# Three quarters of one weight block loaded as 20 rows by a transfer of its own

## The chip, the cores and the metric

The kernel runs on one core of a Trainium2 chip. The metric is device time in microseconds (us) of one launch. Arrays are laid out on the host beforehand; that layout is not part of the time. Everything is float32.

## What is computed

One decoding step for 8 sequences with a model width of 512. A layer norm of `x` feeds two branches: attention of 32 query heads over a cache with 8 key and value heads of 4096 positions, and a small gated MLP whose output, through a silu, multiplies the attention's output. The change touches the last product of the MLP, `z1 * g` (8 x 896) times `w_out` (896 x 512).

```python
def _B_ref(x, w_in, w_sp, b_sp, w_out):
    z = _gelu(jnp.einsum("bsd,df->bsf", x, w_in))
    z1 = z[..., :Fh]
    z2 = _layernorm(z[..., Fh:], axis=-1)
    g = jnp.einsum("ts,bsf->btf", w_sp, z2) + b_sp[None, :, None]
    return jnp.einsum("bsf,fd->bsd", z1 * g, w_out)

x = A_x
xn = _layernorm(x, axis=-1)
s = _A_ref(xn, A_k_cache, A_v_cache, A_wq, A_wo)
g = _silu(_B_ref(xn, B_w_in, B_w_sp, B_b_sp, B_w_out))
return x + s * g
```

`_A_ref` is softmax attention: queries `xn @ wq`, keys and values from the caches, then the product with `wo`. The caches are 8 x 8 x 4096 x 128 each, 134 MB each, and are read once.

## The kernel before

**Data in.** Three buffers of 128 partitions x 64 KB, `slot_A`, `slot_B` and `slot_C`, take everything large. All large loads are issued by SyncE (SP) in the order of the program: `wq` into B (8 MB, L338), `w_mlp` into C (L341), then for each of the eight key/value heads the two halves of the keys into A and B (L547, 8 MB each) and the two halves of the values into C and B (L553). In the last head the first half of the values goes into A, C takes `wo` (L558) in seven pieces that get smaller, and the second half of the values comes in two parts. `x` comes in two pieces on ScalarE's queue (L335): each is 8 rows of 1152 bytes. SP issues a load once the engines that read the old contents of its buffer are done; SP keeps its order, so a load behind a waiting one waits too.

**`w_mlp`.** 128 rows of 10752 numbers: first `w_in` (L342), then the seven blocks of `w_out` side by side (L343), each 128 rows x 512 columns.

**Order of the work.** A small recorder writes down every operation, finds which must wait for which, and emits each engine's program: heads 0 to 6 as a loop on TensorE (PE), the other engines unrolled. Before the heads stand `project_q` twice (L415 to L423, queries from `wq`) and `mlp` (from L431). In `mlp`, PE multiplies by `w_in` (L437); VectorE (DVE), ScalarE and GpSimd make the gelu, the layer norm and the gate (L441 to L467); two transposes (L470) and a copy (L471) bring the hidden vector into `hT`; seven matrix products with the blocks of `w_out` (L474) accumulate in the four row groups of the bank `sc`; DVE copies the result (L476) and the rest makes `gate`. Block j is added in row group j mod 4, so the last block, j = 6, goes to group 2.

**After `mlp`.** Each head computes scores from the keys in A and then in B (L506), softmax (L510 to L529), and the products with the values (L538, with L540, L541 and L544 behind each sequence). The load of the first values into C (L553) may be issued once the last product with `w_out` is done, since they take that buffer's place.

**The end.** The last head folds in the product with `wo` (L566, L574); the last of the seven pieces is awaited by the last 16 matrix products of L574, after which two DVE operations (L630, L631) and the store of the result (L632) remain.

Of the kernel before, what the change touches and what calls it, by code (L numbers as in the profile page):

```python
# [15 lines left out]
P = 128  # L16
B, D = 8, 512
HKV, REP, S, DH = 8, 4, 4096, 128
NK = D // P
G = 4  # L20
J = S // (G * P)
R = 32
FH = 896
FQ = 256
NB = FH // P
# [13 lines left out]
E = 2  # L39
W = P // E  # L40
BANK = 512


class Region:


    def __init__(self, ap):
# [10 lines left out]
        if str(ap.space) == "PSUM" or "PSUM" in str(ap.space):  # L58
            self.p0, self.p1 = 0, P
            banks = np.unique(at // BANK)  # L60
            at = (banks[:, None] * BANK + np.arange(BANK)[None, :]).reshape(-1)
        at = np.unique(at)
# [254 lines left out]
        return self.rec.add(self.eng, "tensor_tensor", (out, a, b), {"op": ALU.subtract})  # L317


def gqa_gmlp_decode(real, x, kT, v, wq, wo, w_mlp, out):  # L320
    nc = Recorder(real)

    def sb(name, shape, **kw):
        return real.alloc_sbuf_tensor(name, shape, F32, **kw).ap()

    def psum(name, shape):
        return real.alloc_psum_tensor(name, shape, F32).ap()

    slots = {n: sb(f"slot_{n}", [P, SLOT], align_bytes=ALIGN) for n in "ABC"}
    pbuf = sb("pbuf", [P, J * P])  # L330
    tbuf = sb("tbuf", [P, B * J * G * REP])
# [5 lines left out]

    nc.sync.dma_start(slots["B"], wq, key="B")  # L338
    wq_sb = slots["B"].rearrange("p (k n) -> p k n", k=NK)
    n_in, n_mlp = NK * 2 * FH, NK * 2 * FH + NB * D  # L340
    nc.sync.dma_start(slots["C"][:, :n_mlp], w_mlp, key="C")  # L341
    w_in_sb = slots["C"][:, :n_in].rearrange("p (k n) -> p k n", k=NK)  # L342
    w_out_sb = slots["C"][:, n_in:n_mlp].rearrange("p (j d) -> p j d", d=D)  # L343

    ident = sb("ident", [P, P])
    make_identity(nc, ident)
# [27 lines left out]
    def shift(t, i):  # L374
        lo = (E - 1 - i) * B
        return t[:, lo:lo + R]

    sc = psum("sc", [P, 2, 512])
    o_ps = [psum(f"o_ps{i}", [P, G, DH]) for i in range(2)]
    po = psum("po", [P, 512])[:, :B * REP]  # L380
    scr = [psum(f"scr{i}", [P, 512]) for i in range(3)]
# [17 lines left out]
    for i in range(E):  # L399
        for g in range(G):  # L400
            lo = g * P + i * W
            nc.tensor.matmul(px[R * g:R * (g + 1), :W], shift(same8, i)[:B], x_sb[:, lo:lo + W],
                             start=(i == 0), stop=(i == E - 1))
# [21 lines left out]
    def mlp():  # L425
        zu = pbuf.rearrange("p (a f) -> p a f", f=FQ)
        z, u = zu[:, :2], zu[:, 2:]
        hT = tbuf[:, :2 * P].rearrange("p (a s) -> p a s", a=2)
        y_sb, e = tbuf[:, 2 * P:2 * P + D], zu[:, 2, :W]
        pz = scr[1]  # L430
        nc.vector.memset(pz, 0.0)  # L431
        for part in range(2):
            for k in range(NK):
                for g in range(G):
                    lo = g * FQ
                    n = min(FQ, FH - lo)
                    nc.tensor.matmul(pz[R * g:R * (g + 1), part * FQ:part * FQ + n], xnT[:, k, :],  # L437
                                     w_in_sb[:, k, part * FH + lo:part * FH + lo + n],
                                     start=(k == 0), stop=(k == NK - 1))
        zf, uf = z.rearrange("p a f -> p (a f)"), u.rearrange("p a f -> p (a f)")  # L440
        nc.vector.tensor_copy(zf, pz)  # L441
        nc.vector.tensor_mul(uf, zf, zf)
        nc.vector.tensor_scalar(uf, uf, 0.044715, 1.0, op0=ALU.mult, op1=ALU.add)
        nc.vector.tensor_mul(uf, uf, zf)
        nc.scalar.activation(uf, uf, AF.Tanh, scale=GELU_C)
        nc.vector.tensor_scalar(uf, uf, 1.0, 0.5, op0=ALU.add, op1=ALU.mult)
        nc.vector.tensor_mul(zf, uf, zf)

        def mean(src, pm, name):
            part_sum, t = sb(f"{name}_sum", [P, 1]), sb(name, [P, 1])  # L450
            nc.vector.tensor_reduce(part_sum, src, op=ALU.add, axis=AX.X)
            nc.tensor.matmul(pm, same_all, part_sum, start=True, stop=True)
            nc.vector.tensor_scalar(t, pm, 1.0 / FH, None, op0=ALU.mult)
            return t

        z1, z2 = z[:, 0, :], z[:, 1, :]
        mu = mean(z2, scr[0][:, :1], "mu")
        nc.vector.tensor_scalar(z2, z2, mu, None, op0=ALU.subtract)
        nc.vector.tensor_mul(u[:, 0, :], z2, z2)
        nc.vector.memset(u[(G - 1) * R:, 0, FH - (G - 1) * FQ:], 0.0)  # L460
        var = mean(u[:, 0, :], scr[2][:, :1], "var")
        nc.vector.tensor_scalar(var, var, EPS, None, op0=ALU.add)
        rs = sb("rs", [P, 1])
        nc.gpsimd.tensor_tensor(rs, var, neg_half, op=ALU.pow)
        nc.vector.tensor_scalar(z2, z2, rs, None, op0=ALU.mult)
        nc.vector.tensor_scalar(z2, z2, wb[:, 0:1], wb[:, 1:2], op0=ALU.mult, op1=ALU.add)
        nc.vector.tensor_mul(u[:, 1, :], z2, z1)  # L467
        th = scr[0][:, :2 * P]
        for a in range(2):
            nc.tensor.transpose(th[:, a * P:(a + 1) * P], u[:, 1, a * P:(a + 1) * P], ident)  # L470
        nc.vector.tensor_copy(hT.rearrange("p a s -> p (a s)"), th)  # L471
        for j in range(NB):
            g = j % G
            nc.tensor.matmul(sc[R * g:R * (g + 1), 0, :], hT[:, j % 2, R * (j // 2):R * (j // 2 + 1)],  # L474
                             w_out_sb[:, j, :], start=(j < G), stop=(j + G >= NB))
        nc.vector.tensor_copy(y_sb, sc[:, 0, :])  # L476
        py = scr[2][:, :W]
        for i in range(E):
            for g in range(G):
                lo = g * P + i * W  # L480
                nc.tensor.matmul(py[R * g:R * (g + 1), :], shift(same8, i), y_sb[:, lo:lo + W],
                                 start=(i == 0), stop=(i == E - 1))
        nc.vector.tensor_scalar(e, py, -1.0, 87.0, op0=ALU.mult, op1=ALU.min)
        nc.scalar.activation(e, e, AF.Exp)
        nc.vector.tensor_scalar(e, e, 1.0, None, op0=ALU.add)
        nc.vector.reciprocal(e, e)
        nc.vector.tensor_mul(gate, py, e)
# [7 lines left out]
    p = pbuf.rearrange("p (j s) -> p j s", j=J)  # L495
# [112 lines left out]
    project_q(0)  # L608
    project_q(1)
    mlp()  # L610
    nc.meet("tensor")
    for h in range(LOOPED):
# [9 lines left out]
    for i in range(E):  # L622
        for g in range(G):
            lo = g * P + i * W
            nc.tensor.matmul(acc[R * g:R * (g + 1), :], shift(same8, i), part_sb[:, lo:lo + W],
                             start=False, stop=False)
# [38 lines left out]
```

## Time and profile before

| what | value |
|---|---|
| time, median of 3 runs | 678.63 us (678.46 to 678.76) |
| the profiled execution, first to last instruction | 677.3 us |
| read from HBM | 290.74 MB |
| PE busy, DVE busy | 375.2 us (55%), 167.5 us (25%) |
| last load: issue to landing | 628.26 us to 674.72 us |

The span is that of one profiled execution; the median of the runs, with what lies around the span, is 1.3 us longer, and differences are carried from the one to the other. A row "DMA" gives the mean busy share of the core's 16 DMA engines, the units that move the bytes. Queues are named q1, q8 and so on: q1 are the loads from SP, q10 those from ScalarE, and the two of the kind "instruction" bring the engines' own programs. Such a row has packets, megabytes and the share of 16 engines' time. In a row "DMA packets ... under 512 B n" for a stretch of time without stores, the packets under 512 bytes are the 4-byte ones by which each DMA engine reports that its share of a transfer is done: their number is the number of engines that came to an end in that stretch.

### The profile page before, as it was taken

The page shows a single profiled execution, that of the slowest core. Times are in us where ns is not written, and L with a number is a line of the kernel's source. Part 1 is how long each engine was busy: PE and PEld are TensorE (multiplying, and loading weights), DVE is VectorE, ACT ScalarE, POOL GpSimd, SP SyncE. Part 2 cuts the span into 40 slices and gives each one's busy share as a digit, 9 for nine tenths or more (in the row PEclk, how much of TensorE's full clock was granted, in tenths as well). Part 3 has the DMA queues.
Part 4 walks back from the last instruction along what each step waited for, and adds up shares of the span by engine and source line. Part 5 has one row for each costly group of instructions (what it writes and reads, how often), then busy time and mean ns, then how long its engine had stood idle before and what let it go on. Part 6 is the DMA issues. An engine that isn't in the chain of part 4 may idle for free. (4 is left out here: it accounts for less than half of the span.)

```text
span 677.3 us, 5857 instructions
## 1 busy us (share of the span) xinstructions
PE 375.2 (55%) x2658; PEld 119.5 (18%) x2658; DVE 167.5 (25%) x277; ACT 13.4 (2%) x27; POOL 2.8 (0%) x14
## 2 busy tenths in 40 slices
PE   0547554546665455456755454655654465655657
PEld 0122121112111111111211121211211121111212
DVE  2141042302430033401521024401432024400342
ACT  0000000000000000000000000000000000000000
POOL 1000000000000000000000000000000000000000
PEclk9967666878767678877766678887676678766697
DMA  8999999999999999999999999999999999999997
GB/s 373 449 434 434 433 434 433 434 433 433 433 433 433 433 433 433 434 433 433 433 433 433 433 434 433 433 433 437 437 437 437 433 437 445 433 437 434 404 423 318
DMA packets 6233, 290.90 MB, mean 429 GB/s; under 512 B 832, under 2 KB 848, under 8 KB 1360
## 3 DMA queue, kind: packets, MB, share of 16 engines
q1 hardware_dynamic: 6192, 290.75, 99.3%
q8 instruction: 7, 0.11, 0.1%
q10 hardware_dynamic: 32, 0.02, 0.0%
q14 instruction: 2, 0.02, 0.0%
HBM read 290.74 MB, written 0.03 MB: 429 GB/s over the span
## 5 line engine op out<-in xcount | busy, mean ns | idle before, releaser
L506 PE MATMUL sc<-slot_B,qz 128*32 128x512 f32 x512 | 74.4, 746 | 76.6 <-PEq L506 76.6
L538 PE MATMUL o_ps<-slot_B,tbuf 128*16 128x512 f32 x512 | 77.5, 732 | 70.5 <-PEq L538 61.6
L506 PE MATMUL sc<-slot_A,qz 128*32 128x512 f32 x512 | 74.4, 746 | 47.6 <-PEq L506 47.6
L540 DVE TENSOR_TENSOR o_all<-o_ps,diag 128x512 f32<-128x512 f32 x64 | 44.3, 691 | 161.0 <-PE o_ps L538 161.0
L538 PE MATMUL o_ps<-slot_C,tbuf 128*16 128x512 f32 x448 | 67.0, 739 | 20.5 <-PEq L538 20.5
L510 DVE TENSOR_REDUCE nm<-sc 128x1 f32<-128x1024 f32 x8 | 9.8, 1224 | 269.5 <-PE sc L506 269.5
L541 DVE TENSOR_REDUCE o_sb<-o_all 128x128 f32<-128x512 f32 x64 | 67.8, 1060 | 2.2
L506 PEld LDWEIGHTS sc<-slot_B,qz 128*32 128x32 f32 x512 | 20.4, 134 | 130.5 <-issue 130.5
L506 PEld LDWEIGHTS sc<-slot_A,qz 128*32 128x32 f32 x512 | 20.7, 133 | 94.8 <-issue 94.8
L544 PE MATMUL po<-fold,o_sb 128*128 128x4 f32 x128 | 25.6, 270 | 12.3 <-PEq L544 12.3
L544 PEld LDWEIGHTS po<-fold,o_sb 128*128 128x128 f32 x128 | 20.3, 199 | 68.5 <-issue 64.2
L538 PEld LDWEIGHTS o_ps<-slot_B,tbuf 128*16 128x16 f32 x512 | 13.4, 106 | 100.5 <-issue 90.2
L538 PEld LDWEIGHTS o_ps<-slot_C,tbuf 128*16 128x16 f32 x448 | 13.7, 112 | 57.0 <-issue 56.8
L528 PE MATMUL scr<-ident,pbuf 128*128 128x128 f32 x64 | 14.8, 409 | 10.6 <-PEq L528 9.3
L511 ACT ACTIVATE pbuf<-sc,nm 128x1024 f32<-128x1024 f32 x8 | 8.9, 1114 | 556.1 <-DVE nm L510 556.1
L528 PEld LDWEIGHTS scr<-ident,pbuf 128*128 128x128 f32 x64 | 11.8, 211 | 11.0 <-issue 9.7
L529 DVE COPY tbuf<-scr 128x512 f32<-128x512 f32 x16 | 11.1, 692 | 10.6 <-PE scr L528 10.6
L415 PE MATMUL scr<-slot_B,xnT 128*32 128x512 f32 x64 | 9.0, 713 | 8.2 <-PEq L415 8.2
L538 PE MATMUL o_ps<-slot_A,tbuf 128*16 128x512 f32 x64 | 9.8, 753 | 3.9 <-PEq L538 3.9
L514 PE MATMUL scr<-ident,nm 128*1 128x128 f32 x8 | 2.2, 269 | 11.8 <-PEq L514 10.4
L394 PE MATMUL scr<-ident,tbuf 8*128 8x8 f32 x4 | 0.6, 255 | 12.9 <-DVE tbuf L391 12.9
L521 PE MATMUL scr<-wl,same 128*128 128x1 f32 x16 | 3.5, 286 | 6.1 <-PEq L521 5.4
(102 smaller groups left out, 88.4 us busy)
## 6 DMA issues: line engine op xcount, KB each, us to landing
slot_B<-in_v SPq DMA_DIRECT2D x2, 4096.0 KB, 33.8
slot_C<-in_w_mlp SPq DMA_DIRECT2D x1, 5376.0 KB, 34.2
slot_C<-in_wo SPq DMA_DIRECT2D x1, 3072.0 KB, 35.4
slot_C<-in_wo SPq DMA_DIRECT2D x1, 2048.0 KB, 41.4
slot_C<-in_wo SPq DMA_DIRECT2D x1, 1280.0 KB, 44.0
slot_C<-in_wo SPq DMA_DIRECT2D x1, 768.0 KB, 45.4
slot_C<-in_wo SPq DMA_DIRECT2D x1, 512.0 KB, 46.1
slot_C<-in_wo SPq DMA_DIRECT2D x2, 256.0 KB, 46.4
```

Source lines behind the costliest of these rows:

```text
L415: nc.tensor.matmul(pq[R * g:R * (g + 1), :], xnT[:, k, :], wq_sb[:, k, lo:lo + REP * DH], start=(k == 0), stop=(k == NK - 1))
L506: nc.tensor.matmul(sc[R * g:R * (g + 1), c, :], qz[:, b * R:(b + 1) * R], k_sb[:, i, c, g, :], start=(b == 0), stop=(b == B - 1))
L510: nc.vector.tensor_reduce(nm, sc, op=ALU.max, axis=AX.XY, negate=True)
L511: nc.scalar.activation(p.rearrange("p j s -> p (j s)"), sc.rearrange("p c s -> p (c s)"), AF.Exp, bias=nm, accum_out=l)
L514: nc.tensor.transpose(a, nm, ident)
L521: nc.tensor.matmul(tot, same_all, wl, start=True, stop=True)
L528: nc.tensor.transpose(t[:, j * P:(j + 1) * P], p[:, 4 * c + j, :], ident)
L529: nc.vector.tensor_copy(pT[:, :, 4 * c:4 * c + 4].rearrange("p b j (g r) -> p (j g) b r", g=G), t.rearrange("p (m b r) -> p m b r", b=B, r ...
L538: nc.tensor.matmul(of[R * c:R * c + G * REP, :], pT[:, b, j, :], v_unit[:, j], start=(j < G), stop=(j >= J - G))
L540: nc.vector.tensor_mul(o_all[b % 2], o, diag[:, :, None].to_broadcast([P, G, DH]))
L541: nc.vector.tensor_reduce(o_sb[b % 2], o_all[b % 2].rearrange("p g d -> p d g"), op=ALU.add, axis=AX.X)
L544: nc.tensor.matmul(po[:, b * REP:(b + 1) * REP], o_sb[b % 2], fold, start=True, stop=True)
```

## The change

384 of the 512 columns of the last `w_out` block leave `w_mlp` (its rows get 10368 numbers instead of 10752) and come in an array of their own, `w_ext`. The block's 128 rows are cut into seven chunks of 20 rows, the last padded from 8; row r of all seven chunks stands side by side, so that `w_ext` has 20 rows of 7 x 384 = 2688 numbers (10752 bytes). On the host these are stored as five groups of four rows with a fifth, unused row in each, and SP loads the four of each (L348 of the changed kernel) into partitions 0 to 19 of `slot_C`, behind `w_mlp`. The hidden vector's 128 numbers for that block are transposed a second time, in chunks of 20, into `hX`, and seven products of depth 20 (the last of 8) take the place of three quarters of one of depth 128.

```diff
+XG, XR, XN = 5, 4, 384
+XK = XG * XR
+XC = -(-P // XK)
+LAST = NB - 1
...
-    n_in, n_mlp = NK * 2 * FH, NK * 2 * FH + NB * D
+    n_in, n_mlp = NK * 2 * FH, NK * 2 * FH + NB * D - XN
     nc.sync.dma_start(slots["C"][:, :n_mlp], w_mlp, key="C")
     w_in_sb = slots["C"][:, :n_in].rearrange("p (k n) -> p k n", k=NK)
-    w_out_sb = slots["C"][:, n_in:n_mlp].rearrange("p (j d) -> p j d", d=D)
+    ext = slots["C"][:XK, n_mlp:n_mlp + XC * XN]
+    nc.sync.dma_start(ext, w_ext[:, :XR])
+    w_ext_sb = ext.rearrange("p (c d) -> p c d", d=XN)
+
+    def w_out_sb(j):
+        return slots["C"][:, n_in + j * D:min(n_in + (j + 1) * D, n_mlp)]
...
         nc.vector.tensor_copy(hT.rearrange("p a s -> p (a s)"), th)
+        low, rows = R * (LAST // 2), [min(XK, P - c * XK) for c in range(XC)]
+        hX = tbuf[:, 2 * P + D:2 * P + D + XC * R].rearrange("p (c r) -> p c r", r=R)
+        tx = scr[2][:, :XC * R].rearrange("p (c r) -> p c r", r=R)
+        for c, n in enumerate(rows):
+            nc.tensor.transpose(tx[:n, c, :], u[low:low + R, 1, (LAST % 2) * P + c * XK:][:, :n],
+                                ident[low:low + R, low:low + R])
+        for n in sorted(set(rows), reverse=True):
+            lo, hi = rows.index(n), rows.index(n) + rows.count(n)
+            nc.vector.tensor_copy(hX[:n, lo:hi], tx[:n, lo:hi])
         for j in range(NB):
             g = j % G
-            nc.tensor.matmul(sc[R * g:R * (g + 1), 0, :], hT[:, j % 2, R * (j // 2):R * (j // 2 + 1)],
-                             w_out_sb[:, j, :], start=(j < G), stop=(j + G >= NB))
+            w_j = w_out_sb(j)
+            nc.tensor.matmul(sc[R * g:R * (g + 1), 0, :w_j.shape[1]], hT[:, j % 2, R * (j // 2):R * (j // 2 + 1)],
+                             w_j, start=(j < G), stop=(j + G >= NB and j < LAST))
+        for c, n in enumerate(rows):
+            g = LAST % G
+            nc.tensor.matmul(sc[R * g:R * (g + 1), 0, D - XN:], hX[:n, c, :], w_ext_sb[:n, c, :],
+                             start=False, stop=(c == XC - 1))
...
+    w_out = c(B_w_out).reshape(NB, P, D)
+    w_ext = np.zeros((XC * XK, XN), np.float32)
+    w_ext[:P] = w_out[LAST, :, D - XN:]
+    w_ext = w_ext.reshape(XC, XG, XR, XN).transpose(1, 2, 0, 3).reshape(XG, XR, XC * XN)
+    w_ext = np.concatenate([w_ext, np.zeros((XG, 1, XC * XN), np.float32)], axis=1)
```

On SP's queue the new load stands between `w_mlp` and the first keys. SP's first loads before:

```order
L338 DMA slot_B<-in_wq 128x16384
L341 DMA slot_C<-in_w_mlp 128x10752
L547 DMA slot_A<-in_kT 128x16384
L547 DMA slot_B<-in_kT 128x16384
L553 DMA slot_C<-in_v 128x16384
```

and with the change:

```order
L342 DMA slot_B<-in_wq 128x16384
L345 DMA slot_C<-in_w_mlp 128x10368
L348 DMA slot_C<-in_w_ext 20x1x2688
L571 DMA slot_A<-in_kT 128x16384
L571 DMA slot_B<-in_kT 128x16384
L577 DMA slot_C<-in_v 128x16384
```

One load more is issued ahead of everything but `wq` and `w_mlp`. On PE, at the end of `mlp` and up to the first scores, before:

```order
L470 MATMUL scr<-ident,pbuf 128x128 x2
L474 MATMUL sc<-slot_C,tbuf 32x512 x7
L481 MATMUL scr<-tbuf,same 32x64 x8
L288 UNCONDITIONAL_BRANCH
L506 MATMUL sc<-slot_A,qz 32x512 x32
```

and with the change:

```order
L480 MATMUL scr<-ident,pbuf 128x128 x2
L486 MATMUL scr<-ident,pbuf 20x32 x6
L486 MATMUL scr<-ident,pbuf 8x32
L494 MATMUL sc<-slot_C,tbuf 32x512 x6
L494 MATMUL sc<-slot_C,tbuf 32x128
L498 MATMUL sc<-slot_C,tbuf 32x384 x7
L505 MATMUL scr<-tbuf,same 32x64 x8
L292 UNCONDITIONAL_BRANCH
L530 MATMUL sc<-slot_A,qz 32x512 x32
```

Seven transposes (L486) come in ahead of the products with `w_out`, and seven products of 384 columns (L498) behind them. From there on PE's program is the same but for line numbers.

More of the change, by code (lines that the diff above doesn't have):

```diff
@@ L317, in tensor_sub, with gqa_gmlp_decode @@
         return self.rec.add(self.eng, "tensor_tensor", (out, a, b), {"op": ALU.subtract})
-def gqa_gmlp_decode(real, x, kT, v, wq, wo, w_mlp, out):
+def gqa_gmlp_decode(real, x, kT, v, wq, wo, w_mlp, w_ext, out):
     nc = Recorder(real)
@@ L646 @@
     vv = c(A_v_cache).reshape(2, HALF, HKV, P, J, G, DH)
+    w_out = c(B_w_out).reshape(NB, P, D)
+    w_mlp = np.concatenate([
+        c(B_w_in).reshape(NK, P, 2 * FH).transpose(1, 0, 2).reshape(P, NK * 2 * FH),
+        c(w_out.transpose(1, 0, 2)).reshape(P, NB * D)], axis=1)
+    w_ext = np.zeros((XC * XK, XN), np.float32)
+    w_ext[:P] = w_out[LAST, :, D - XN:]
+    w_ext = w_ext.reshape(XC, XG, XR, XN).transpose(1, 2, 0, 3).reshape(XG, XR, XC * XN)
+    w_ext = np.concatenate([w_ext, np.zeros((XG, 1, XC * XN), np.float32)], axis=1)
     arrays = {
@@ L652 @@
         "wo": c(c(A_wo).reshape(HKV * REP, P, D).transpose(1, 0, 2)).reshape(P, SLOT),
-        "w_mlp": np.concatenate([
-            c(B_w_in).reshape(NK, P, 2 * FH).transpose(1, 0, 2).reshape(P, NK * 2 * FH),
-            c(B_w_out).reshape(NB, P, D).transpose(1, 0, 2).reshape(P, NB * D)], axis=1),
+        "w_mlp": c(w_mlp[:, :NK * 2 * FH + NB * D - XN]),
+        "w_ext": w_ext,
     }
```

## The prediction

> **What bounds the kernel now.** I read the page first: the span, the row of the DMA engines in 40 slices, and the queues.
>
> ```profile
> span 677.3 us, 5857 instructions
> DMA  8999999999999999999999999999999999999997
> q1 hardware_dynamic: 6192, 290.75, 99.3%
> q8 instruction: 7, 0.11, 0.1%
> q10 hardware_dynamic: 32, 0.02, 0.0%
> q14 instruction: 2, 0.02, 0.0%
> ```
>
> SP's loads on q1 alone fill 99.3% of what 16 DMA engines can do in the span. So the bytes set the time, not PE or DVE. The second view is the chain of waits, which ends in a load; beside it a row of the stages gives the rate in the long middle.
>
> ```profile
> 628.26 46.46 DMA slot_C<-in_wo
> 674.72 0.04 issue
> 674.76 0.47 PE sc L574 x16
> ```
>
> ```profile
> 100.00:600.00 500.00, 276.40 (x1832) 85.64 (x1836) 125.19 (x185) 8.45 (x18) 0.00 (x0) 0.74 1.00 434
> ```
>
> The last piece of `wo` lands at 674.72 us and everything after it is a fixed tail. At a share of 1.00 the 16 engines move 434 GB/s, so one engine moves 434 / 16 = 27.1 GB/s, or 27.1 KB per us. A load is over when its slowest engine is: what matters is not the mean but **the last of the 16 engines**. The third view, the DMA rows of short stretches, counts how many engines report the end of one and the same load early and late. Here are four loads, two stretches each (the first load needs one: all 16 within 21.5 to 23); the stretches are 21.5 to 23, then 53 to 55 and 55 to 57, 613.5 to 615.2 and 615.2 to 617, 659.8 to 661 and 661 to 662.6. Below them stand the rows of the instruction queue for 30 to 50 and for 673.2 to 673.8 us.
>
> ```profile
> DMA packets 32, 0.69 MB, mean 459 GB/s; under 512 B 16, under 2 KB 16, under 8 KB 16
> ...
> DMA packets 31, 1.05 MB, mean 524 GB/s; under 512 B 15, under 2 KB 15, under 8 KB 15
> ...
> DMA packets 17, 1.05 MB, mean 524 GB/s; under 512 B 1, under 2 KB 1, under 8 KB 1
> ...
> DMA packets 24, 0.85 MB, mean 501 GB/s; under 512 B 11, under 2 KB 11, under 8 KB 11
> ...
> DMA packets 19, 0.92 MB, mean 510 GB/s; under 512 B 5, under 2 KB 5, under 8 KB 5
> ...
> DMA packets 33, 0.51 MB, mean 423 GB/s; under 512 B 9, under 2 KB 9, under 8 KB 9
> ...
> DMA packets 41, 0.56 MB, mean 348 GB/s; under 512 B 7, under 2 KB 7, under 8 KB 7
> ```
>
> ```profile
> q8 instruction: 1, 0.02, 0.3%
> ...
> q8 instruction: 1, 0.02, 11.6%
> ```
>
> Late engines: 0, 1, 5, 7. The page counts 7 + 2 = 9 instruction packets in the whole run; one of them, between 30 and 50 us, lies between the load with no late engine and the one with one. I read it so: every instruction packet makes one engine fall behind for good: it has to carry the packet beside its equal share of the loads. Nine packets but seven late engines: one packet comes only at 673.2 to 673.8, and one must have hit an engine that was late already. That engine is probably the last of all. How far apart the groups are at the very end, the stages show:
>
> ```profile
> 672.00:672.40 0.40, 0.40 (x8) 0.11 (x4) 0.00 (x0) 0.00 (x0) 0.00 (x0) 1.00 1.04 415
> 672.40:672.80 0.40, 0.40 (x32) 0.39 (x28) 0.14 (x1) 0.00 (x0) 0.00 (x0) 1.00 0.64 251
> 672.80:673.20 0.40, 0.40 (x45) 0.40 (x37) 0.40 (x1) 0.00 (x0) 0.00 (x0) 1.00 0.48 184
> 673.60:674.00 0.40, 0.40 (x36) 0.40 (x40) 0.00 (x0) 0.00 (x0) 0.00 (x0) 1.00 0.45 174
> 674.00:674.40 0.40, 0.40 (x44) 0.40 (x32) 0.00 (x0) 0.00 (x0) 0.00 (x0) 1.00 0.18 67
> ```
>
> The DMA share (the last number but one) falls from 1.04 to 0.48 by 672.8 and stays there: 0.48 x 16 is about 8 engines still at work, the other 8 are done at about 672.7. The landing at 674.72 is thus some 2.0 us after the early half.
>
> **The change, part by part.** *Bytes.* `w_mlp` loses 128 x 384 x 4 = 196,608 bytes, 12,288 on each of 16 engines: 12.29 / 27.1 = 0.45 us less for each. `w_ext` brings 20 x 10,752 = 215,040 bytes. How many engines carry them? `x` is loaded in two pieces of 8 rows, and q10 has 32 packets for both: per piece 8 rows and 8 reports, so 8 rows go to 8 engines, while the 128-row loads above show 16 reports. The number of engines follows the outermost count; here that is 5 groups of 4 rows. I take five engines with four rows each, 43,008 bytes: 43.0 / 27.1 = 1.59 us more, net 1.59 - 0.45 = +1.13 us on five engines and -0.45 us on eleven. The bounds: all 16 would be 215,040 / 16 = 13,440 bytes each, net +0.04 us; a single engine 215.0 / 27.1 = 7.93, net +7.5 us on it.
>
> The Trainium skill, "DMA: Bandwidth & Descriptors", section "Why a DMA increments its semaphore by 16 and not by 1", says that the engines used are the largest number up to 16 that divides the slowest dimension of both sides, and for loads from SP the lowest-numbered ones; by it 5 (source) and 20 (destination) give engines 0 to 4, and the sum is the same.
>
> *Which five.* If all five are of the early group, they finish at 672.7 + 1.13 = 673.8, and the last engine at 674.72 - 0.45 = 674.27 remains the last: the landing is **0.45 us earlier**. If one of the five is the last engine, the landing is 674.72 + 1.13 = 675.85. If one is another late engine the landing lies in between. No view groups packets by engine. Lining up the packet starts in the trace (an engine's data packets follow each other without a gap), I find the eight engines that carried `x` to be seven early ones and the one that took both packets of q14; the q8 packets are on engines that carried no `x`. By number alone the five lowest of eight leave out a given one in 3 of 8 cases; but among the eight this engine was seventh to begin its first data packet and last to go on after its second `x` packet, which speaks for a high number. I take 0.6 for left out.
>
> *Does the tail follow?* PE must be ready when the data comes earlier. The timeline:
>
> ```profile
> 662.49 3.61 PE L538 MATMUL o_ps<-slot_B,tbuf 128*16 128x512 f32 x16 [5.30 <-DMA slot_B<-in_v]
> 674.76 0.43 PE L574 MATMUL sc<-slot_C,oT_end 128*32 128x64 f32 x16 [0.16 <-DMA slot_C<-in_wo]
> ```
>
> At the last wait PE is only 0.16 us ahead, so it is nearly bound itself. But its run of work from 662.49 starts upon the landing of the second part of the values, which comes earlier by the same 0.45 us. I take the full 0.45; if PE's granted clock falls otherwise, the gain is 0.16 us at the least.
>
> *PE and DVE in `mlp`.* The rows around it:
>
> ```profile
> 51.56 0.69 PE L470 MATMUL scr<-ident,pbuf 128*128 128x128 f32 x2 [2.38 <-DVE pbuf L467]
> 52.28 0.42 DVE L471 COPY tbuf<-scr 128x256 f32<-128x256 f32 x1 [0.78 <-PE scr L470]
> 52.76 3.64 PE L474 MATMUL sc<-slot_C,tbuf 128*32 128x512 f32 x14 [0.52 <-DVE tbuf L471]
> 56.45 0.33 SPq L553 DMA_DIRECT2D slot_C<-in_v  x1
> 59.68 8.77 PE L506 MATMUL sc<-slot_A,qz 128*32 128x512 f32 x64 [2.05 <-PEq L506]
> 75.51 9.73 PE L506 MATMUL sc<-slot_B,qz 128*32 128x512 f32 x64 [7.06 <-PEq L506]
> ```
>
> Seven products become 6 of 512, one of 128 and 7 of 384 columns: 3072 + 128 + 2688 = 5888 columns for 3584, so 3.64 x 5888 / 3584 = 5.98 us, +2.34. Seven transposes at 0.69 / 2 each are at most +2.4 us. The two new copies (no larger than L471's 0.42 us each) run beside the products. Together up to +5.2 us, on the path to the scores from A. That ends at 59.68 + 8.77 = 68.45 and may slip by 7.06 us before the scores from B at 75.51, which wait for their keys, are touched. The load of the values into C, issued at 56.45, slips as much; the 8.4 MB of keys issued ahead of it, for which the scores at 75.51 waited, keep the engines at work until nearly then, so no engine runs dry: 0. Without that cover it would cost up to 5.2 us.
>
> *SP's queue.* The page has the load of `w_mlp`, issued among the first:
>
> ```profile
> slot_C<-in_w_mlp SPq DMA_DIRECT2D x1, 5376.0 KB, 34.2
> ```
>
> One more issue, 0.33 us like L553's, comes in front of the first keys. `wq` and `w_mlp`, 8.4 + 5.3 MB, give the engines over 30 us of work by then: 0. The wait of the first chunk product for `w_ext` ends at about 1.1 us after `w_mlp`'s landing 34.2 us behind its issue, so near 37 us, and the products come after 52: 0. The products and the gate behind it on PE wait no longer for it.
>
> *Instruction packets.* PE's program grows by 14 transpose and 28 product instructions net; its packets come a little earlier, and I see no reason for another engine to take them. DVE gains two copies.
>
> Sum: 0.45 us off the span; 678.63 - 0.45 = **678.2 us** as the median of the runs.
>
> **The rivals.** (1) *The last engine is among the five.* The doubly hit engine gets +1.13 us, every load from then on lands with it, and SP, PE and the store follow: 678.63 + 1.13 = 679.8 us, slower than before. It decides as soon as an engine that ended less than 1.13 us before 674.72 is one of the five; then the loss is 1.13 minus its lead. For it: the engine with both q14 packets lies among the eight that `x` uses. Against: its late start among them. The Trainium skill's rule on the same page, in "Rules for kernel authors", "Use all 16 engines", warns that an outermost count under 16 confines a transfer to that many engines; it speaks for this rival, and the 8 reports per piece of `x` agree with it as to the count.
>
> (2) *The 20 rows go to one or two engines.* One engine: 672.7 + 7.5 = 680.2 at the least if it is an early one, 5.5 us after 674.72: 684.1 us. Two: 3.97 - 0.45 = +3.5 us, landing at 676.2 at least, 680.1 us or more. Against it: the 8 rows of `x` on 8 engines.
>
> (3) *The rows spread over all 16.* Then nothing moves off the late engines: +0.04 us, 678.7 us. Against it: the same rows of `x`.
>
> (4) *A further instruction packet on the last engine*, of q14's kind, for the two added copies or SP's added load. At 8 KB it is 0.3 us of an engine, and the gap to the early group (2.0 us for one or two packets) says that it may cost about 1 us in all: 678.2 + 1 = 679.2 us. Against it: DVE's program grows by under 1%.
>
> **How the numbers follow.** The forecast has 0.6, rival 1 has 0.2, rivals 2 to 4 have 0.07, 0.06 and 0.05, and 0.02 is left for what I do not see. The predicted time is the likeliest case, 678.2 us; its own range is 677.9 to 678.5 (the PE bound of 0.16 us above, the scatter of the runs of 0.15 us on both sides). The range with 8 in 10 reaches to rival 1: 677.9 to 679.9. A measurement of this kernel tells about 0.2%, 1.36 us, from no change: faster means under 677.3, slower over 680.0. The forecast, rivals 1, 3 and 4 lie between. Slower are rival 2 and the upper part of rival 1 with a further delay, 0.14 in all; faster would take three times the forecast gain: 0.03; within: 0.83.
>
> **What would show it.** Right: q1's bytes up by 0.02 MB; the new load reporting from five engines; at the end fewer engines early and the fall of the DMA share in one step near 674 instead of a long half-busy stretch; last landing near 674.3. Wrong: the last landing near 675.8 with the half-busy stretch longer (rival 1); one or two engines at work for several us after the others (rival 2); an unchanged picture (rival 3); more than nine instruction packets (rival 4). If the scores from B begin later than the keys' landing, or the DMA share dips between 70 and 100 us, the cover in `mlp` was misjudged.

## The result and the profile after

The changed kernel takes 679.7 us (median of 21 runs, 679.47 to 680.37) against 678.6 us before (21 runs, 678.33 to 678.82): ratio 1.0017, 95% interval 1.0011 to 1.0023. It is 1.1 us slower. The forecast of the prediction was 0.45 us faster; the time is that of its rival 1, 679.8 us. It lies inside the stated range, and the direction was wrong.

The queues of the profile after (packets, MB, share of 16 engines' time):

```profile
span 678.4 us, 5903 instructions
...
DMA packets 6258, 290.92 MB, mean 429 GB/s; under 512 B 837, under 2 KB 853, under 8 KB 1365
...
q1 hardware_dynamic: 6217, 290.77, 99.1%
q8 instruction: 7, 0.11, 0.1%
q10 hardware_dynamic: 32, 0.02, 0.0%
q14 instruction: 2, 0.02, 0.0%
```

q1 has 25 packets more than before: the 20 rows of `w_ext` and 5 reports (the small packets go from 832 to 837). So five engines carried the rows, as the prediction took it. There are still nine instruction packets. The chain of waits of the kernel after, as before, ends in the last piece of `wo`:

```profile
630.13 45.70 DMA slot_C<-in_wo
675.83 0.04 issue
675.88 0.47 PE sc L598 x16
```

It lands at 675.83 us, 1.11 us later than the 674.72 before; rival 1 had 675.85. The reports of the load of the second part of the values, for 659.8 to 660.8, 660.8 to 662.3 and 662.3 to 664 us:

```profile
DMA packets 24, 0.48 MB, mean 475 GB/s; under 512 B 5, under 2 KB 5, under 8 KB 5
...
DMA packets 42, 0.56 MB, mean 371 GB/s; under 512 B 10, under 2 KB 10, under 8 KB 10
...
DMA packets 47, 0.75 MB, mean 443 GB/s; under 512 B 1, under 2 KB 1, under 8 KB 1
```

Before there were two groups, 9 early and 7 late. Now 5 are early, 10 are in the middle, and one comes alone behind them. That is what four early engines and one late engine with rows would give: 9 - 4 = 5 stay early, the four join six late ones, and the fifth is alone. The last stages show the same engine (the last but one column is the DMA share):

```profile
673.60:674.00 0.40, 0.40 (x44) 0.40 (x36) 0.00 (x0) 0.00 (x0) 0.00 (x0) 1.00 0.36 138
674.00:674.40 0.40, 0.25 (x20) 0.09 (x8) 0.00 (x0) 0.00 (x0) 0.00 (x0) 1.00 0.05 20
674.40:674.80 0.40, 0.20 (x13) 0.20 (x17) 0.00 (x0) 0.00 (x0) 0.00 (x0) 1.00 0.07 26
674.80:675.20 0.40, 0.40 (x43) 0.40 (x37) 0.00 (x0) 0.00 (x0) 0.00 (x0) 1.00 0.07 26
675.20:675.60 0.40, 0.40 (x36) 0.34 (x25) 0.00 (x0) 0.00 (x0) 0.00 (x0) 1.00 0.05 20
```

A share of 0.07 is 1.1 of 16 engines: for the last 1.6 us one engine alone moves data (26 GB/s, one engine's rate), and the whole kernel waits for it. The rows went to five engines, and one of these was the engine that had no time.

In `mlp` the added work of PE is there and hidden:

```profile
52.34 3.63 PE L494 MATMUL sc<-slot_C,tbuf 128*32 128x512 f32 x14
55.90 5.80 PE L498 MATMUL sc<-slot_C,tbuf 20*32 20x384 f32 x14
61.74 0.33 SPq L577 DMA_DIRECT2D slot_C<-in_v  x1
...
75.02 5.36 PE L530 MATMUL sc<-slot_B,qz 128*32 128x512 f32 x48 [0.44 <-PEq L530]
```

The values' load is issued at 61.74 instead of 56.45, 5.3 us later, and the scores from B begin at 75.02 instead of 75.51. Of the 7.06 us by which PE waited there, 0.44 is left: the scores from A began 5.5 us later and took 0.6 us longer, and the keys for B came 0.5 us earlier. The cover held, but hardly more work would have fitted under it.

### The profile page after: what moved, and what is told of

Same layout as the page of the kernel before. It is cut to its first block, busy times and chain, and to the rows that moved or that the text cites. A ratio compares the mean times of both kernels' runs of the same rounds, so it can differ in the third digit from the quotient of the medians.

```text
span 678.4 us, 5903 instructions
## 1 busy us (share of the span) xinstructions
PE 379.0 (56%) x2679; PEld 127.5 (19%) x2679; DVE 168.0 (25%) x279; ACT 13.4 (2%) x27; POOL 2.8 (0%) x14
## 5 line engine op out<-in xcount | busy, mean ns | idle before, releaser
L562 PE MATMUL o_ps<-slot_C,tbuf 128*16 128x512 f32 x448 | 68.4, 753 | 23.8 <-PEq L562 23.8
L530 PEld LDWEIGHTS sc<-slot_A,qz 128*32 128x32 f32 x512 | 26.4, 132 | 89.9 <-issue 87.7
```

What stands on the lines that cost most here:

```text
L530: nc.tensor.matmul(sc[R * g:R * (g + 1), c, :], qz[:, b * R:(b + 1) * R], k_sb[:, i, c, g, :], start=(b == 0), stop=(b == B - 1))
L562: nc.tensor.matmul(of[R * c:R * c + G * REP, :], pT[:, b, j, :], v_unit[:, j], start=(j < G), stop=(j >= J - G))
```

## The experiments

All are compared with the kernel before on the same chip; "the q14 engine" is the DMA engine that takes both instruction packets of q14. Theory A: it is one of the five, and it alone sets the loss. The rivals: B, the chunked products cost the time; C, a load on few engines costs as such; D, reads around the small load are disturbed.

**Other numbers of groups.** Only the constants change; the number of groups decides the number of engines (4 x 4 rows of 320 columns, 3 x 6 of 192, 2 x 8 of 128, 16 x 1 of 384).

```diff
-XG, XR, XN = 5, 4, 384
+XG, XR, XN = 4, 4, 320
```

> The 384 columns come as eight chunks of 16 rows, sixteen groups of one row, so that all 16 DMA engines should carry 12,288 bytes each, as much as they lose from w_mlp; the smaller products stay. Theory A (the loss comes from one DMA engine, the one with both q14 packets, which is among the five): no engine gets more, so 678.6 us, within 0.3 of before. Rival B (the chunked products or the further instructions cost the time): still about 679.7 us. Rival C (the loss comes from a load on few engines as such, whichever they are): 678.6 us as well.

> Four groups of four rows, 320 columns: four engines get 40,960 bytes and all lose 10,240, net +1.13 us on four and -0.38 us on twelve. Theory A: if the engine with both q14 packets is the fifth, 678.6 - 0.4 = 678.2 us; if it is one of the first four, 679.7 us. Rival B: about 679.7 us. Rival C: 679.7 us.

> Three groups of six rows, 192 columns: three engines get 36,864 bytes and all lose 6,144, net +1.13 us on three and -0.23 us on thirteen. Theory A: 678.4 us if the engine with both q14 packets is the fourth or fifth, 679.7 us if it is one of the first three. Rival B: about 679.7 us. Rival C: 679.7 us.

> Two groups of eight rows, 128 columns: two engines get 32,768 bytes and all lose 4,096, net +1.06 us on two and -0.15 us on fourteen. Theory A: 678.5 us if the engine with both q14 packets is the third to fifth, 679.7 us if it is one of the first two. Rival B: about 679.7 us. Rival C: 679.7 us.

| run | groups | time, us (kernel before in the same session: 678.61) | ratio, 95% interval |
|---|---|---|---|
| k16 | 16 | 680.51 | 1.0035 (1.0021 to 1.0049) |
| k4 | 4 | 679.90 | 1.0020 (1.0011 to 1.0029) |
| k3 | 3 | 679.25 | 1.0012 (1.0003 to 1.0021) |
| k2 | 2 | 678.99 | 1.0007 (0.9998 to 1.0016) |

Here and below a time is a median, and the ratio is not the quotient of two medians. These runs did not settle it. k4 is where A puts it if the q14 engine is among the first four, but C foresaw the same; k3 lies between the two answers, and k16 was to be as before and is the slowest of all. In k16, k3 and k2 the trace has long packets of the keys just behind the small load, which theory A does not have: the first of all 16 engines took 2.7 to 3.8 us in k16, three packets 2.7 to 3.2 us in k3 and three 2.8 to 2.9 us in k2. In k4 and in the changed kernel all took 2.42 us. So the next runs leave the products alone.

**A load more, nothing else.** The kernel before gets one load that nothing reads, with the shape of the change's: rows of 10,752 bytes in 5, 4 or 3 groups of four, taken from `w_mlp`.

```diff
     w_out_sb = slots["C"][:, n_in:n_mlp].rearrange("p (j d) -> p j d", d=D)
+    more = w_mlp[:25].rearrange("(g r) n -> g r n", r=5)[:, :4, :2688]
+    nc.sync.dma_start(slots["C"][:20, n_mlp:n_mlp + 2688], more)
```

> The kernel before with one load more that nothing reads: 20 rows of 10,752 bytes in five groups of four, into unused columns of slot_C; no product is changed. Five DMA engines get 1.59 us more, none gets less. Theory A (the engine with both q14 packets is the fourth by number, so it is among the five): 678.6 + 1.6 = 680.2 us. Rival B (the chunked products cost the time of the change): 678.6 us, since the other engines end 1.6 us or more ahead. Rival D (the five are early ones, and it is the disturbed reads around the small load that cost): anything between 678.6 and 679.3 us, and the same for the three runs with a further load.

> The same with 16 rows in four groups of four: four engines get 1.59 us more. Theory A: the fourth engine is among them, 680.2 us. Rival B: 678.6 us. Rival D: as with five groups.

> The same with 12 rows in three groups of four: three engines get 1.59 us more. Theory A: the fourth engine is not among them and the three end early, so 678.6 us, at most 0.3 more for disturbed reads. Rival B: 678.6 us. Rival C (any load on few engines costs): 680.2 us. Rival D: as with five groups.

| run | engines that carry it | time, us (before: 678.75) | ratio, 95% interval |
|---|---|---|---|
| more5 | 5 | 680.08 | 1.0020 (1.0011 to 1.0029) |
| more4 | 4 | 680.14 | 1.0021 (1.0012 to 1.0030) |
| more3 | 3 | 678.56 | 0.9998 (0.9989 to 1.0007) |

The last landing in the chain of waits of more4, and then of more3:

```profile
630.08 46.41 DMA slot_C<-in_wo
676.49 0.04 issue
```

```profile
628.81 45.73 DMA slot_C<-in_wo
674.54 0.04 issue
```

The profiled execution of more4 took 680.40 us, the longest of its eleven, so its landing is later than the median would give. The medians are theory A as written down, to about 0.2 us. The same 43,008 bytes for each engine cost 1.3 to 1.4 us when four or five engines carry them and nothing when three do. There is no chunked product in these kernels and the loss is there all the same, so B falls as the cause; three engines are fewer than four, so C falls; D has the three runs alike, and in the changed kernel no packet behind the small load was long, so it falls as well. What differs between more4 and more3 is the fourth group of rows.

The Trainium skill, "DMA: Bandwidth & Descriptors", section "Why a DMA increments its semaphore by 16 and not by 1", has such a load on the lowest-numbered engines; by it the fourth would be engine 3. The step from more3 to more4 agrees with sets that contain each other; that the engines are the lowest-numbered ones no run here shows.

That the fourth engine is the q14 engine, and not one that was late through a q8 packet, can be read from the packet starts, since an engine's next packet follows the last without a gap. In more4 a q14 packet starts at 402.154 us, the data packet behind it ends at 405.415, and that engine's report, at 405.412, is the last of the 16, 1.60 us behind the next. The queue row for 402.15 to 402.16 us of more4 (the packet outlasts so short a stretch, hence a share over 100%) and the packets for 403.82 to 405.5 us, with the one report in them:

```profile
q14 instruction: 1, 0.01, 193.1%
...
DMA packets 10, 0.59 MB, mean 351 GB/s; under 512 B 1, under 2 KB 1, under 8 KB 1
```

In the changed kernel the q14 engine is alone in the same way, 1.64 us behind the next (404.761 against 403.125). In the kernel before it is the last by 0.24 us only (403.647 against 403.411), in more3 by 0.07 us (422.776 against 422.705).

**A longer program for DVE.** To see that an instruction packet sets the last engine, 60 memsets of one number are added on DVE where it waits anyway; no load is touched.

```diff
+    idle = sb("idle", [1, 1])
+    for _ in range(30):
+        nc.vector.memset(idle, 0.0)
     st, mv, rstd = sb("st", [B, 6]), sb("mv", [B, 2]), sb("rstd", [B, 2])
...
     q_sb = pbuf[:, :REP * DH]
+    for _ in range(30):
+        nc.vector.memset(idle, 0.0)
```

> The kernel before with 60 more memsets of one number on DVE, 30 while it waits for x and 30 while it waits for the queries' product; no load is changed. DVE's program grows past a further block, so that a third q14 packet should come near 550 us. Theory A: it hits the engine that has had the other two, which is the last, and costs it 0.84 us as each of them did: 679.4 us. If it hits another engine, or the packets don't set the last engine: 678.6 us.

Measured: 679.42 us against 678.75, ratio 1.0010 (1.0001 to 1.0019). The row of q14 for 560 to 575 us, where the kernel before has no such packet, and the last landing in the chain of waits:

```profile
q14 instruction: 1, 0.01, 0.1%
```

```profile
630.13 45.39 DMA slot_C<-in_wo
675.52 0.04 issue
```

The third packet has come (the other two now come at 19.4 and 245.8 us instead of 90.5 and 400.4), and the landing is 0.80 us later than before (675.52 against 674.72). The 0.84 us that were expected can be read in the trace of the kernel before: from the start of the q14 packet at 400.397 to the end of the data packet behind it at 403.651 are 3.25 us, where a data packet by itself takes 2.42. A packet of 8 KB is 0.3 us of one engine's rate and costs 0.8 us. Since only DVE's program grew, q14 brings that program; and since the last landing moved by about the full price, the packet came to the engine that was the last already.

**The change with three groups.** With the q14 engine known to be the fourth, the change is repeated on three engines, with a row length like the change's, eleven chunks of 12 rows, and `hX` in a buffer of its own, since eleven chunks do not fit in `tbuf`.

```diff
-XG, XR, XN = 5, 4, 384
+XG, XR, XN = 3, 4, 256
...
-        hX = tbuf[:, 2 * P + D:2 * P + D + XC * R].rearrange("p (c r) -> p c r", r=R)
+        hX = sb("hX", [P, XC * R]).rearrange("p (c r) -> p c r", r=R)
```

> The change with three groups of four rows (12 rows of 11,264 bytes, 256 columns, eleven chunks) and hX in a place of its own: the engine with the q14 packets gets no row and loses 8,192 bytes, 0.30 us. Theory A: 678.6 - 0.3 = 678.3 us, up to 678.6 if reads around the small load are disturbed as in k2 and k3. Rival B: about 679.7 us or more, since there are more chunks.

Measured: 678.54 us against 678.64, ratio 0.9999 (0.9990 to 1.0008). Theory A computes a gain of 0.30 us; in the runs it cannot be told from nothing. In the one profiled execution (678.36 us, shorter than the median) the last landing is:

```profile
628.36 46.08 DMA slot_C<-in_wo
674.43 0.04 issue
```

That is 0.29 us earlier than before, as computed, but the runs scatter by as much, so the gain is not shown. More chunks than in the change, and no loss: B falls a second time. No version here beats the kernel before by more than can be measured.

**Why sixteen groups are slow.** k16 was meant as a harmless control. Three runs ask what cost it: other row lengths and distances (k16b: 336 columns), and the kernel before with one further row of 10,752 bytes for each of 16 engines, out of `w_mlp` (more16) or out of a small array (more16s).

```diff
+    more = w_mlp[:32].rearrange("(g r) n -> g r n", r=2)[:, :1, :2688]
+    nc.sync.dma_start(slots["C"][:16, n_mlp:n_mlp + 2688], more)
```

In k16b only the number of columns differs from k16; in more16s the rows are those of an array of 16 x 2 x 2688 zeros, the first of each two.

> As k16, but 336 columns in place of 384, so that a row of the small load has 10,752 bytes and the rows lie 21,504 bytes apart instead of 24,576; still sixteen groups of one row, still eight chunks and the smaller products. If the loss of k16 came from where its rows lie in memory (all 16 DMA engines read slowly there and behind it), 678.6 us, within 0.4 of before. If it came from sixteen engines reading one small array at once, about 680 us again. Rival B (the chunked products cost the time): about 680 us too; the trace tells the two apart by the length of the first 65,536-byte packets behind the small load.

> The kernel before with one load more that nothing reads: 16 rows of 10,752 bytes out of w_mlp, 86,016 bytes apart, one to each of the 16 DMA engines; no product is changed. Bytes alone: 10,752 more for each engine, 0.40 us, so 679.0 us. If sixteen engines upon a small load disturb the reads behind it as in k16 and k16b, 1.2 us more: 680.2 us.

> The same 16 rows out of a small array of their own, 21,504 bytes apart as in k16b. Bytes alone 679.0 us. If it is the small array that is read slowly, 680.2 us here and 679.0 us in more16; if the chunked products were what cost k16 and k16b their time (rival B), 679.0 us in both and no long packets behind the small load.

| run | time, us (before) | ratio, 95% interval |
|---|---|---|
| k16b | 680.11 (678.64) | 1.0021 (1.0012 to 1.0030) |
| more16 | 680.53 (678.71) | 1.0041 (1.0018 to 1.0064) |
| more16s | 680.39 (678.71) | 1.0026 (1.0016 to 1.0036) |

Stages of 2 us around the small load, of more3 and then of more16; the last two columns, the DMA share and the rate, count a packet where it begins:

```profile
34.00:36.00 2.00, 0.66 (x4) 0.42 (x4) 1.14 (x6) 0.00 (x0) 0.00 (x0) 1.00 1.14 491
36.00:38.00 2.00, 1.53 (x31) 1.08 (x34) 0.41 (x1) 0.00 (x0) 0.00 (x0) 1.00 1.21 524
```

```profile
34.00:36.00 2.00, 0.66 (x4) 0.42 (x4) 1.15 (x6) 0.00 (x0) 0.00 (x0) 1.00 1.92 578
36.00:38.00 2.00, 1.40 (x22) 1.06 (x26) 0.04 (x1) 0.00 (x0) 0.00 (x0) 0.77 0.09 33
```

From 36 to 38 us more16 begins one packet in all (33 GB/s for 2 us is 65,536 bytes); the 16 engines are still at the first packets of the keys, which otherwise take 2.42 us each and here took 2.7 to 3.6 us. So with one row for each of 16 engines in front of the keys, all 16 read slowly for once. The small array and the chunked products are ruled out: more16 has neither and loses as much, 1.8 us, of which 10,752 bytes are 0.40. The distance of the rows made no clear difference among the three that were run: 24,576 bytes in k16, 21,504 in k16b and more16s, 86,016 in more16. Why the reads slow down stays open; more16 differs from more3 both in the number of engines and in the rows for each, and no run parts the two. k3 showed some long packets at the same place in one profile; I put the larger part of its loss there, but that was not tested, and neither was the 0.4 us of k2, whose interval contains no change.

## Why the prediction was wrong

**The step that failed is "Which five".** The prediction had narrowed it to one question, whether the q14 engine is among the five, and took 0.6 for "left out". more4 and more3 show that it is the fourth of them: the engine that sets the end got +1.13 us and not -0.45, and the landing moved by +1.11. The reason for 0.6 was the order in which the engines began their first packets and went on after `x`; here that order pointed the wrong way. The count that stood beside it, 3 of 8 for left out, needed no such reading and would have made rival 1 the likeliest. A weak sign was let outweigh the plain count. The chances do not agree with each other either: 0.6 for left out leaves 0.4 for among the five, but rival 1 was given 0.2.

**Right, by its own steps.** *The bound*: the last of 16 engines, not the mean; the share of 0.07 at the end is that engine alone. *The instruction packets*: each makes one engine late for good; dve60 adds one of q14 and gets 0.80 us. (In the stages at the end the share does not quite stay at 0.48: the row left out there, 673.2 to 673.6 us, has 0.63, with the last instruction packet in it.) *The sum of bytes*: five engines, by packets and reports; +1.13 us on an engine that has no lead was 675.85 for the landing, 675.83 is measured, and 679.8 us for the time, 679.7 measured. *The doubly hit engine is the last one*: the lone engine after is the one with the q14 packets, 1.6 us behind the others. *The tail follows*: the span grew by 1.1 us like the landing. *`mlp`, SP's queue*: the delay of the values' load was 5.3 us, a little over the 5.2 foreseen as the most, and it stayed under the cover with 0.44 us to spare. *No further instruction packet*: nine, as before; rivals 2, 3 and 4 did not come.

**A size that was off.** PE's products took 3.63 + 5.80 us, not 5.98. The view by source line has the matrix products, of the kernel before (L474) and of the kernel after (L498), with the shortest, median and longest in ns:

```profile
L474 PE MATMUL sc<-slot_C,tbuf x14: 1061/1061/1062, 52.8 to 55.3; 128*32 128x512 f32 x14
```

```profile
L498 PE MATMUL sc<-slot_C,tbuf x14: 481/481/839, 55.9 to 60.9; 20*32 20x384 f32 x12, 8*32 8x384 f32 x2
```

Each of the seven products stands there as two passes. Fourteen of 1.06 us fitted into 3.64 us before, about four at a time: the blocks go to the four row groups in turn. The chunks all belong to the last block and so to one row group, and fourteen of 0.48 us and more took 5.80 us, fewer than two at a time, although the granted clock was higher (0.79 against 0.50). Scaling by columns missed that. That the one row group is the reason is likely but not shown, since no run spread the chunks over the groups. The seven transposes took 0.54 us in all, while PE would have waited for the copy L481 anyway: the products start 1.20 us behind the first transposes in both kernels, so the up to 2.4 us foreseen for them were nothing. The total came out near by luck, by two errors of opposite sign.

## What to carry to other kernels

When loads bound a kernel, ask for each DMA engine when it is done, not for the mean: moving bytes to few engines helps only if none of these is the last one or becomes it, and a load more that nothing reads, on a growing number of groups, finds that engine in a few runs. Where a forecast hangs on which of several like units is meant and the profile does not name them, keep the plain odds and do not lean on a sign such as the order of their starts. An engine's program is traffic too: in a kernel that is bound by its loads, as this one, a longer program on an engine with time to spare cost 0.67 us.

## What the runs showed that was not expected

One row of 10,752 bytes for each of 16 engines, issued between two large loads, cost 1.8 us where its bytes are 0.40 (more16; more16s 1.7), while four rows for each of three engines cost nothing (more3). And 60 one-number memsets on an idle DVE cost 0.67 us (679.42 against 678.75) by one more 8 KB packet of its program, which takes 0.3 us at one engine's rate and made that engine 0.8 us later.
